# A stack of spectral and token-mixing layers on one Trainium2 core: the last layer's first product, by seven products of quarters

## The chip, the cores and the metric

One core of one Trainium2 chip runs the whole program. Its engines have their own instruction queues and work at the same time: TensorE (PE in the profile; its weight loads are PEld) multiplies matrices, VectorE (DVE) and ScalarE (ACT) do elementwise work, GpSimd (POOL) does some elementwise work and issues transfers, SyncE (SP) only issues transfers. A transfer (DMA) moves data between the chip's memory and the on-chip SBUF. Matmuls write PSUM, which has here four buffers. The metric is the device time of one execution in microseconds, lower is better.

## The reference

Two kinds of layer alternate, A B A B, on x of 2048 tokens by 640 channels. Each adds to x.

```python
def _A_ref(x, w_r, w_i):
    X = rfft2(x); X = X * (w_r + 1j * w_i)
    return irfft2(X, s=(S, D))
def _B_ref(x, w1, b1, w2, b2):
    h = _layernorm(x, axis=-1)
    u = jnp.einsum("bsd,sf->bdf", h, w1) + b1
    u = _gelu(u)
    y = jnp.einsum("bdf,fs->bds", u, w2) + b2
    return y.transpose(0, 2, 1)
x = x + _A_ref(_layernorm(x), A_w_r, A_w_i)
x = x + _B_ref(_layernorm(x), B_w1, B_b1, B_w2, B_b2)
x = x + _A_ref(_layernorm(x), A_w_r, A_w_i)
x = x + _B_ref(_layernorm(x), B_w1, B_b1, B_w2, B_b2)
```

S = 2048, D = 640, F = 1728. All is float32. The two B layers use the same weights. The first product of a B layer is w1 transposed (1728 x 2048) by h (2048 x 640), the second w2 transposed (2048 x 1728) by the GELU of it.

## The kernel before

The kernel gets float32 accuracy out of float16 matmuls: every operand is a high part (float16 of the scaled value) and a low part (float16 of the rest), and `mm3` multiplies high by high, high by low and low by high: three matmuls of 128 x 128 weights by 128 x 320 columns. High parts come from ScalarE, low parts (one subtraction) from VectorE.

`b1st` is the first B layer, `b2nd` the last. The 2048 tokens are 16 row blocks (NJ), the 1728 features 14 tiles of 128 (NFT; tile 13 holds its 64 features twice, so that two matmuls do for three), and the 640 channels two halves of 320. The first product goes tile by tile: per tile 16 row blocks x 2 halves x 3 = 96 matmuls, for tile 13 64. `wload` asks SP for a tile's weights in two transfers of 512 KB, `wsplit` makes the parts, `scan1` and `scale1` (first layer only) find the scale: ScalarE squares and sums the raw tile, VectorE reduces, TensorE adds over partitions.

In `b2nd` SEQ gives the order of the tiles: 0, 7, 6, 13, 1, 8 and so on, so that tiles t and t + 7 follow each other. `both_high` has the first two tiles' products with high parts of h go out early, in gaps of the stage before (`a2`, which makes h, `hf` in float32 and `hh` its high part); the low parts `hl` follow from VectorE. After each tile come bias and GELU, and `usplit` makes the parts of u.

The second product of the last layer (from `PQ`) is already done by quarters, after Strassen and Winograd: for tiles d and d + 8 of the output, the weights are a 2 x 2 block matrix A11, A12, A21, A22 and u a block matrix B11 to B22, and seven products (four sums S1 to S4 of quarters of A, four sums T1 to T4 of quarters of B) do for eight. VectorE forms the S sums (`form`), `hi` and `lo` the parts, three products ahead; `evict` adds a product from PSUM to the results.

The order of the work is the order in which it is written where `self.pin` is set (`Pin`, line 59, is the one line that the profile shows for nearly all operations); elsewhere a planner may move operations by its own estimate. The SP queue works in order: a transfer that must wait for a buffer holds up those behind it. `push` and `pop` open and close pools of SBUF; a tile laid over an older one waits for the older one's last use.

Of the kernel before, what the change touches and what calls it, by code (L numbers as in the profile page):

```python
# [21 lines left out]
NQ = 8  # L22
# [7 lines left out]
SEQ = [t + 7 * i for t in (0, 6, 1, 2, 3, 4, 5) for i in range(2)]  # L30
# [36 lines left out]
class Layers:  # L67
# [41 lines left out]
    def setup(self):  # L109
# [17 lines left out]
        self.s2, self.c2 = (base.tile([128, NQ], F32, name=f"{a}p") for a in "sc")  # L127
        self.second, self.nr = False, 3
# [299 lines left out]
    def a1(self, first):  # L428
# [4 lines left out]
        self.hh = {j: ph.tile([128, 2, 320], F16, name=f"hh{j}_{self.n}") for j in HA}  # L433
# [262 lines left out]
    def a2(self, li):  # L696
# [4 lines left out]
        self.wp[1] = self.push("wb", side=self.sp)  # L701
        ph = self.push("hf", side=self.sp)
        self.hf = [ph.tile([128, 2, 320], F32, name=f"hf{j}_{self.n}") for j in range(NJ)]
# [159 lines left out]

    def b1st(self, li):
# [10 lines left out]
        self.wsplit(1, hi=False)  # L875
        self.wload(2)
# [226 lines left out]
    def usums(self, f, fs, *names):  # L1103

        B11, B12, B21, B22 = (f[:, i] for i in range(4))
        T1, T2, T3, T4 = (fs[:, i] for i in range(4))
        q = {"T1": (T1, B12, B11), "T2": (T2, B22, T1), "T3": (T3, B22, B12), "T4": (T4, B21, T2)}
        for n in names:
            a, b, c = q[n]
            self.V.tensor_tensor(a, b, c, op=ALU.subtract)  # L1110

    def b2nd(self, li):
# [6 lines left out]
        V, T = self.V, self.T  # L1119
        mm = self.PE.matmul  # L1120
        ADD, SUB, MUL = ALU.add, ALU.subtract, ALU.mult
        ph = self.push("h", side=self.sq)
        for j in range(NJ):
            if j not in HA:
                self.hh[j] = ph.tile([128, 2, 320], F16, name=f"hh{j}_{self.n}")
                T.activation(self.hh[j], self.hf[j], AF.Copy)
        self.pin = True
        self.wsplit(1, hi=False)
        self.h = []
        for j in range(NJ):  # L1130
            self.h.append((self.hh[j], ph.tile([128, 2, 320], F16, name=f"hl{j}_{self.n}")))
            V.tensor_tensor(self.h[j][1], self.hf[j], self.hh[j], op=SUB)
        V.tensor_tensor(self.s2, self.st[1][:, :NQ], self.st[1][:, NQ:], op=ALU.min)
        V.tensor_tensor(self.c2, self.ct[1][:, :NQ], self.ct[1][:, NQ:], op=ALU.max)
        self.pin = False
# [3 lines left out]
        px = self.push("px", side=self.sp)  # L1139
        pu = self.push("u", side=self.sp)  # L1140

        u = [pu.tile([128, 2, 7, 320], F16, name=f"u{f}_{self.n}") for f in range(7)]
        p = self.push("b1", side=self.sq)
        for m in (2, 3, 4, 5):
            self.wload(m)

        def ahead(m):

            self.wload(m + 4)
            if m + 1 < NFT:  # L1150
                self.wopen(m + 1)


        PQ = ("A11", "B11"), ("S1", "T1"), ("S2", "T2"), ("S3", "T3"), ("A12", "B21"), ("S4", "B22"), ("A22", "T4")
        UB = {a: i for i, a in enumerate(("B11", "B21", "B22", "T1", "T2", "T3", "T4"))}
        ops = [(d, *q) for d in range(NQ) for q in PQ]
        NP = len(ops)
        places = [(px, f"wo{i}") for i in range(3)] + [(q, a) for q in self.wp for a in ("wh", "wl")]
        src, wo = {}, {}

        def raw(d, a):
            return self.wraws[NFT + 2 * d + int(a[1]) - 1][int(a[2]) - 1]

        def form(n):

            if n >= NP:
                return
            d, a, _ = ops[n]
            if a[0] == "A":
                src[n] = raw(d, a)  # L1170
                return
            s = src[n] = self.t(px, [128, 7, 128], F32, a, 1)
            x, y, op = {
                "S1": ((d, "A21"), (d, "A22"), ADD), "S2": (n - 1, (d, "A11"), SUB),
                "S3": ((d, "A11"), (d, "A21"), SUB), "S4": ((d, "A12"), n - 3, SUB),
            }[a]
            x, y = (src[q] if isinstance(q, int) else raw(*q) for q in (x, y))
            V.tensor_tensor(s, x, y, op=op)

        def hi(n):  # L1180
            if n >= NP:
                return
            q, tag = places[n % 7]
            w = self.t(q, [128, NJ, 128], F16, tag, 1).rearrange("p (a b) c -> p a b c", a=2)[:, :, :7]
            wo[n] = w
            T.activation(w[:, 0], src[n], AF.Identity, scale=self.s2[:, ops[n][0]:][:, :1])

        def lo(n):
            if n >= NP:
                return  # L1190
            w = wo[n]
            V.scalar_tensor_tensor(w[:, 1], src[n], self.s2[:, ops[n][0]:][:, :1], w[:, 0], op0=MUL, op1=SUB)
# [54 lines left out]
        for m in range(NFT):  # L1247
            t, k = SEQ[m] % 7, SEQ[m] // 7
            if m < 2:
                ps, run = pss[m], rest(m, pss[m], w[m])  # L1250
                if m:
                    self.wopen(2)
# [449 lines left out]
```

## Time and profile before

| | us |
|---|---|
| median of 3 runs (1027.93 to 1029.49) | 1028.31 |
| the profiled execution | 1028.95 |
| its span | 1027.2 |
| TensorE busy | 986.3 |
| VectorE busy | 725.5 |
| ScalarE busy | 571.2 |
| GpSimd busy | 265.7 |

In the rows of the profile stand the start in us from the span's start, the duration, the engine, the line, the operation, what it writes and reads, and how many; in brackets the idle time before it and what ended it. Rows of groups give the count, the total, the mean in ns and the idle time before. The chain is the work that ended last, followed back from the end. PEclk is the clock that TensorE was granted, 1.00 in all of the last layer. The last layer's first product lies at about 683 to 864 us, its first matmuls in gaps of the stage before; the second product runs from there to the end.

### The profile page before, as it was taken

How to read it: one execution, taken by the hardware profiler on the slowest of the kernel's cores; microseconds unless marked ns; L12 is line 12 of the kernel's file. 1: busy time of each engine (PE TensorE's matmuls, PEld its weight loads, DVE VectorE, ACT ScalarE, POOL GpSimd, SP SyncE). 2: the span in 40 equal slices, each digit the busy share in tenths (PEclk: the TensorE clock that was granted, in tenths of full speed). 3: DMA queues.
4: the chain of work that ended last, by engine and by line, in shares of the span. 5: the costliest groups of instructions: out<-in, count | busy, mean ns of one | idle time of the engine just before them, and what ended most of it. 6: DMA issues, size and time to landing. Idle time of an engine off the chain costs nothing.

```text
span 1027.2 us, 20943 instructions
## 1 busy us (share of the span) xinstructions
PE 986.3 (96%) x8379; PEld 735.7 (72%) x8379; DVE 725.5 (71%) x1422; ACT 571.2 (56%) x874; POOL 265.7 (26%) x438
## 2 busy tenths in 40 slices
PE   4889999999999999999998999999999999999998
PEld 3768777677777777777776787776777777777776
DVE  7968978954333956666666797897655564988885
ACT  5847768675554556555542575774544454544541
POOL 6927857500000002222222675780000000000000
PEclk9589999999999999999999999999999999999999
DMA  7855356522222264444312644756322232445511
GB/s 230 277 173 168 116 167 222 207 83 99 77 77 74 72 233 155 138 135 123 124 55 86 214 125 130 223 177 210 108 82 83 72 109 77 141 154 175 164 44 52
DMA packets 55738, 139.48 MB, mean 136 GB/s; under 512 B 6461, under 2 KB 12249, under 8 KB 55641
## 3 DMA queue, kind: packets, MB, share of 16 engines
q1 hardware_dynamic: 54200, 131.97, 40.1%
q0 software_dynamic: 1440, 6.17, 2.0%
q8 instruction: 66, 1.08, 0.4%
q14 instruction: 32, 0.25, 0.1%
HBM read 115.05 MB, written 23.07 MB: 134 GB/s over the span
## 4 chain that ended last, share of the span: by engine, by line
PE 76%; DVE 13%; POOL 3%; issue 3%; DMA 2%; ACT 2%; SPq 0%; POOLq 0%; DVEq 0%; ACTq 0%
PE ps L59 76%; DVE st L59 2%; POOL xt L59 2%; DVE xt L59 2%; DVE f L59 1%; DVE Yl L59 1%; DVE s1l L59 1%; DVE hl L59 1%; DVE ta L59 1%; ACT eh L59 1%; DVE el L59 1%; DMA rest<-s1l 1%; POOL r L59 1%; DVE tb L59 1%; DMA stk<-rest 1%
## 5 line engine op out<-in xcount | busy, mean ns | idle before, releaser
L59 PEld LDWEIGHTS <-wh 128*128 128x128 f16 x2992 | 289.7, 98 | 113.4 <-issue 1.8
L59 PEld LDWEIGHTS <-wl 128*128 128x128 f16 x1616 | 157.9, 98 | 62.2 <-DVE wl L59 0.9
L59 PE MATMUL ps<-hh,wh 128*128 128x320 f16 x896 | 186.6, 299 | 0.7 <-ACT hh L59 0.7
L59 PE MATMUL ps<-hl,wh 128*128 128x320 f16 x896 | 184.7, 299 | 0.0
L59 PE MATMUL ps<-hh,wl 128*128 128x320 f16 x832 | 171.4, 299 | 0.6 <-DVE wl L59 0.6
L59 DVE SCALAR_TENSOR_TENSOR wl<-raw,s,wh 128x1024 f16<-128x1024 f32 (+2 forms) x88 | 105.4, 1202 | 87.4 <-ACT wh L59 87.3
L59 PE MATMUL ps<-uh,wl 128*128 128x320 f16 x448 | 133.1, 299 | 0.0
L59 PE MATMUL ps<-ul,wh 128*128 128x320 f16 x448 | 133.1, 299 | 0.0
L59 ACT ACTIVATE wh<-raw,s 128x1024 f16<-128x1024 f32 (+2 forms) x92 | 94.7, 1047 | 68.4 <-PE ps L59 61.6
L59 PE MATMUL ps<-uh,wh 128*128 128x320 f16 x416 | 124.3, 299 | 0.0
L59 ACT ACTIVATE junk<-raw 128x896 bf16<-128x896 f32 (+1 forms) x60 | 59.6, 994 | 46.5 <-DMA raw<-w 46.4
L59 POOL TENSOR_TENSOR r<-v,mh 128x1 f32<-128x1 f32 x64 | 37.4, 584 | 132.2 <-DVE nm L59 122.6
L59 PE MATMUL ps<-tDi,Yh 128*128 128x322 f16 x320 | 71.3, 300 | 0.2
L59 PE MATMUL ps<-u,wo 128*128 128x320 f16 x504 | 69.9, 299 | 0.0
L59 DVE TENSOR_TENSOR f<-eo 128x256 f32<-128x256 f32 (+1 forms) x124 | 39.1, 368 | 38.8 <-POOL eo L59 38.1
L59 PEld LDWEIGHTS <-wo 128*128 128x128 f16 x504 | 49.3, 98 | 19.1
L59 POOL TENSOR_TENSOR xt<-xt,ec 128x320 f32<-128x320 f32 x64 | 52.4, 841 | 32.8 <-DVE xt L59 32.6
L59 PE MATMUL ps<-ph,tS 128*128 128x321 f16 (+2 forms) x288 | 59.6, 289 | 1.3 <-DVE tb L59 1.3
L59 ACT ACTIVATE z<-xt,nb,r 128x640 f32<-128x640 f32 x31 | 28.5, 919 | 55.8 <-POOL z L59 43.5
L59 DVE BATCH_NORM_STATS2 st<-xt 128x6 f32<-128x320 f32 x126 | 55.3, 481 | 5.7 <-DMA xt<-x 4.6
L59 PE MATMUL ps<-tM,f 128*128 128x128 f32 x160 | 39.5, 426 | 19.8 <-DVE f L59 19.8
L59 POOL TENSOR_TENSOR eo<-z 128x320 f32<-128x320 f32 x62 | 53.3, 880 | 17.1 <-ACT z L59 15.1
(174 smaller groups left out, 1877.0 us busy)
## 6 DMA issues: line engine op xcount, KB each, us to landing
raw<-w SPq DMA_DIRECT2D x56, 512.0 KB
xt<-x SPq DMA_DIRECT2D x79, 320.0 KB
w<-w SPq DMA_DIRECT2D x48, 321.0 KB
x<-xt SPq DMA_DIRECT2D x47, 320.0 KB
raw<-w SPq DMA_DIRECT2D x32, 448.0 KB
raw<-w2z SPq DMA_DIRECT2D x32, 448.0 KB
out<-xt SPq DMA_DIRECT2D x15, 320.0 KB
tIM<-tIM POOLq DMA_DIRECT2D x8, 512.0 KB, 5.6
```

The costliest lines, as they stand in the source:

```text
L59: i = f(*a, **k)
```

## The change

The first product of the last layer goes by quarters too. Tile 6 and tile 13 (SEQ is now those two) go as before. The other twelve make six pairs (d, d + 7), each with seven products of 8 row blocks x 3 = 24 matmuls on 320 columns. The quarters A11, A12 and A22 are not loaded as float32 and split: the first layer stores their parts, which it makes anyway, in the chip's memory (`wstore`: both halves of tiles 0 to 5, which are A11 and A12, and the second half of tiles 7 to 12, which is A22), and `fetch` brings them back in one transfer of 512 KB. The sums of weights are made by transfers: SP loads one quarter (`begin`), and GpSimd issues transfers that add others to it in place (`more`). S1 is A21 + A22; when its parts are made, A11 is added to the same buffer, which gives S2, and then A12, which gives S4. S3 is A11 + A21. The signs are taken up by T1 to T4, which VectorE makes in place in `hf` (`tsum`), with parts from `thi` and `tlo`. FIRST, NEXT and LAST1 set the order of the 42 products; `first`, `last` and `stage` hold what goes with each. The loads of w2 for output pair 1 move behind the first product's end, ahead of the first x rows on SP.

```diff
...
-SEQ = [t + 7 * i for t in (0, 6, 1, 2, 3, 4, 5) for i in range(2)]
+SEQ = [6, 13]
...
+        self.s1p, self.c1p, self.c1n = (base.tile([128, 7], F32, name=f"{a}p1") for a in "scn")
+        self.wst = {
+            t: self.dram.tile([128, 2, 2, 8, 128] if t < 6 else [128, 2, 8, 128], F16, name=f"wst{t}")
+            for t in range(NFT - 1) if t != 6
+        }
...
                 V.scalar_tensor_tensor(l, raw, sc, h, op0=ALU.mult, op1=ALU.subtract)
+    def wstore(self, m):
+        if m not in self.wst:
+            return
+        for k, w in enumerate(self.w[m]):
+            q = w.rearrange("p (c b) f -> p c b f", c=2)
+            self.nc.sync.dma_start(*((self.wst[m][:, :, k], q) if m < 6 else (self.wst[m][:, k], q[:, 1])))
...
         self.wsplit(1, hi=False)
+        self.wstore(0)
+        self.wstore(1)
         self.wload(2)
...
             for c in range(2 if m + 1 < NFT + NJ else 0):
                 self.wsplit(m + 1, (c,))
+                if c and m + 1 < NFT:
+                    self.wstore(m + 1)
                 yield
...
+        self.wr[1] = self.push("wr", side=self.sq)
+        px = self.push("px", side=self.sq)
         ph = self.push("h", side=self.sq)
-        for j in range(NJ):
-            if j not in HA:
-                self.hh[j] = ph.tile([128, 2, 320], F16, name=f"hh{j}_{self.n}")
-                T.activation(self.hh[j], self.hf[j], AF.Copy)
-        self.pin = True
-        self.wsplit(1, hi=False)
-        self.h = []
-        for j in range(NJ):
-            self.h.append((self.hh[j], ph.tile([128, 2, 320], F16, name=f"hl{j}_{self.n}")))
...
-        self.pop("hf")
-        self.nr = 4
-        self.wr[1:] = (self.push(a, side=self.sp) for a in ("wr", "wr2", "wr3"))
...
-        for m in (2, 3, 4, 5):
-            self.wload(m)
...
+        hhb, hlb = (ph.tile([128, 8, 2, 320], F16, name=f"{a}b{self.n}") for a in ("hh", "hl"))
+        hl0, hl1 = (q.tile([128, 8, 320], F16, name=f"{a}{self.n}") for q, a in ((ph, "hl0"), (hx, "hl1")))
+        TT = {a: [pt.tile([128, 8, 320], F16, name=f"{a}{b}{self.n}") for b in "hl"] for a in ("T1", "T2", "T3", "T4")}
+        for j in range(8, NJ):
+            T.activation(hhb[:, j - 8], hf[j], AF.Copy)
...
+        P1 = {"A11": "B11", "S1": "T1", "S2": "T2", "A12": "B21", "S3": "T3", "S4": "B22", "A22": "T4"}
+        P2 = {"A11": "B11", "S1": "T1", "S2": "T2", "S3": "T3", "A12": "B21", "S4": "B22", "A22": "T4"}
+        ND = 6
+        FIRST = "A11.0 A12.0 A11.1 A12.1 S1.0 S2.0 S3.0 S4.0 A22.0 S1.1 S1.2 A11.2 S2.1 S3.1 A22.1 S4.1 A12.2 S2.2 S3.2 A22.2 S4.2"
+        NEXT, LAST1 = "S1 A11 A12 S2 S3 A22 S4", "S1 A11 A12 S2 S3 S4 A22"
+        ops = [(int(q[-1]), q[:-2], P1[q[:-2]]) for q in FIRST.split()]
+        ops += [(d, q, P1[q]) for d in range(3, ND) for q in (NEXT if d < ND - 1 else LAST1).split()]
+        N1 = len(ops)
+        at = {(d, a): n for n, (d, a, _) in enumerate(ops)}
+        ops += [(d, *q) for d in range(NQ) for q in P2.items()]
...
+        places = [(px, "wo0"), (px, "wo1"), (self.wp[0], "wl"), (self.wp[1], "wl"), (self.wp[0], "wh"), (self.wp[1], "wh")]
+        w1 = lambda d, a: A["w1"][d + 7 * (a[1] == "2")][:, 8 * int(a[2]) - 8:8 * int(a[2])]
+        w2 = lambda d, a: A["w2z"][d + NQ * (a[1] == "2")][:, 7 * int(a[2]) - 7:7 * int(a[2])]
+        def raw(pool, tag, n, q):
+            return self.t(pool, [128, 8, 128], F32, tag, n)[:, :q]
+        def begin(d, a):
+            pool, tag = (self.wr[1], "Sa") if a == "S1" else (self.wr[0], "raw")
+            cur[d, a] = raw(pool, tag, 2, 8)
+            nc.sync.dma_start(cur[d, a], w1(d, "A21" if a == "S1" else "A11"))
+        def more(d, a, b):
+            G.dma_start(cur[d, a], w1(d, b), accum_op=ADD)
+        def place(n, k):
+            q, tag = places[n % len(places)]
+            w = self.t(q, [128, NJ, 128], F16, tag, 1)
+            w = wo[n] = w[:, :2 * k].rearrange("p (a b) c -> p a b c", a=2)
+            return w
+        def fetch(n):
+            if n < N1 and ops[n][1][0] == "A":
+                d, a, _ = ops[n]
+                nc.sync.dma_start(place(n, 8), self.wst[d][:, int(a[2]) - 1] if a[1] == "1" else self.wst[d + 7])
...
         def hi(n):
...
-            q, tag = places[n % 7]
-            w = self.t(q, [128, NJ, 128], F16, tag, 1).rearrange("p (a b) c -> p a b c", a=2)[:, :, :7]
-            wo[n] = w
-            T.activation(w[:, 0], src[n], AF.Identity, scale=self.s2[:, ops[n][0]:][:, :1])
+            d, a, _ = ops[n]
+            if n < N1:
+                if a[0] == "A":
+                    return
+                src[n] = cur[d, "S3" if a == "S3" else "S1"]
+            elif a[0] == "A" and n not in src:
+                form(n)
+            w = place(n, 8 if n < N1 else 7)
+            T.activation(w[:, 0], src[n], AF.Identity, scale=scale(n))
...
         def lo(n):
-            if n >= NP:
+            d, a, _ = ops[min(n, NP - 1)]
+            if n >= NP or n < N1 and a[0] == "A":
                 return
             w = wo[n]
-            V.scalar_tensor_tensor(w[:, 1], src[n], self.s2[:, ops[n][0]:][:, :1], w[:, 0], op0=MUL, op1=SUB)
-        def prep(m):
+            V.scalar_tensor_tensor(w[:, 1], src[n], scale(n), w[:, 0], op0=MUL, op1=SUB)
+            if n < N1 and a in ("S1", "S2"):
+                more(d, "S1", "A11" if a == "S1" else "A12")
...
+        def tsum(a, c, W=V):
+            j, k = slice(4 * c, 4 * c + 4), slice(8 + 4 * c, 12 + 4 * c)
+            B11, B12, B21, B22 = hfa[:, j, 0], hfa[:, j, 1], hfa[:, k, 0], hfa[:, k, 1]
+            o, x, y = {"T1": (B12, B12, B11), "T2": (B22, B22, B12), "T3": (B11, B22, B11), "T4": (B21, B21, B22)}[a]
+            W.tensor_tensor(o, x, y, op=SUB)
...
+        def thi(a):
             for c in range(2):
-                if m + 1 < NFT:
-                    self.wsplit(m + 1, (c,))
-                yield
+                T.activation(TT[a][0][:, 4 * c:4 * c + 4], tsrc(a, c), AF.Copy)
+        def tlo(a):
+            for c in range(2):
+                j = slice(4 * c, 4 * c + 4)
+                V.tensor_tensor(TT[a][1][:, j], tsrc(a, c), TT[a][0][:, j], op=SUB)
+        def hlow(c):
+            j = slice(4 * c % 8, 4 * c % 8 + 4)
+            if c < 2:
+                V.tensor_tensor(hl0[:, j], hfa[:, j, 0], hha[:, j, 0], op=SUB)
+                V.tensor_tensor(hl1[:, j], hfa[:, j, 1], hha[:, j, 1], op=SUB)
+            else:
+                V.tensor_tensor(hlb[:, j], hfa[:, 4 * c:4 * c + 4], hhb[:, j], op=SUB)
...
+        def product(n):
+            d, a, b = ops[n]
+            o = bank[d, a] = self.big()[:, 0, :320]
+            w = wo[n]
+            for j in range(8):
+                self.mm3(o, (w[:, 0, j], w[:, 1, j]), operand(b, j), j == 0, j == 7)
...
+        for d in range(ND):
+            i = {a: at[d, a] for a in P1}
+            for q in P1:
+                if i[q] < N1 - 1:
+                    first[i[q] + 1].append(lam(evict, d, q))
...
+        for d in range(1, ND):
+            n, k = at[d, "S1"], at[d, "S3"]
+            stage[max(n - 6, 0)].append(lam(begin, d, "S1"))
+            stage[max(n - 5, 0)].append(lam(more, d, "S1", "A22"))
+            stage[max(k - 7, 0)].append(lam(begin, d, "S3"))
+            stage[max(k - 6, 0)].append(lam(more, d, "S3", "A21"))
+        def load2(d, a, pool=None, tag=None, n=2):
+            raws[d, a] = raw(pool, tag, n, 7)
+            nc.sync.dma_start(raws[d, a], w2(d, a))
+        for n, a, pool, tag in (
+            (N1 - 9, "A21", self.wr[1], "Sa"), (N1 - 9, "A22", self.wr[0], "raw"), (N1 - 5, "A11", self.wr[0], "raw"),
+            (N1 - 4, "A12", self.wr[1], "Sa"),
+        ):
+            stage[n].append(lam(load2, 0, a, pool, tag))
...
+        self.pin = True
+        fetch(0)
+        fetch(1)
+        begin(0, "S1")
+        more(0, "S1", "A22")
+        self.wsplit(1, hi=False)
+        begin(0, "S3")
+        more(0, "S3", "A21")
...
+        for js in (early, late):
+            prod(pss[0], wh0, hhigh, js, start=True)
+            prod(pss[0], wl0, hhigh, js)
+            prod(pss[1], wh1, hhigh, js, start=True)
+        fetch(2)
+        fetch(3)
+        hlow(0)
+        hlow(1)
+        for i, w in enumerate((wh0, wh1)):
+            prod(pss[i], w, hlows, low)
+        product(0)
+        hlow(2)
+        hlow(3)
+        for i, w in enumerate((wh0, wh1)):
+            prod(pss[i], w, hlows, high, stop=True)
+        for a in ("T1", "T2"):
+            for c in range(2):
+                tsum(a, c)
+        thi("T1")
+        hi(4)
+        tlo("T1")
+        lo(4)
+        thi("T2")
+        tlo("T2")
+        self.pop("hx")
+        p = self.push("b1", side=self.sq)
+        pr = self.push("br", side=self.sp)
+        f = pr.tile([128, 4, 320], F32, name=f"fr{self.n}")
+        q0, q1 = (pr.tile([128, 2, 320], F32, name=f"qr{k}{self.n}") for k in range(2))
+        t0, t1 = SEQ
+        pv, bb, cc = pss[0][:, :, :320], self.b1[:, t0:t0 + 1], self.ct[0][:, t0:t0 + 1]
+        T.activation(f[:, A2], pv, AF.Identity, scale=cc, bias=bb)
+        T.activation(q0, pv, AF.Square, scale=cc, bias=bb)
+        pv, sw = pss[1][:, :, :320], f[:, A4]
+        T.activation(sw[:64], pv[64:], AF.Copy)
+        T.activation(sw[64:], pv[:64], AF.Copy)
+        V.tensor_tensor(sw, pv, sw, op=ADD)
...
+        for n in range(1, N1):
+            product(n)
+            for e in first[n]:
+                e()
+            if n == 2:
+                hi(5)
+                lo(5)
+            if n > 2:
+                hi(n + 3)
+                lo(n + 3)
+            for e in last[n]:
+                e()
+            for e in stage[n]:
+                e()
+            fetch(n + 4)
+        f5, q2 = fs[D5], q5[1][:, 0]
+        evict(D5, "A22")
...
         self.pop("b1")
+        self.pop("T")
         self.pop("h")
-        self.pop("ha")
         p = self.push("b2", side=self.sq)
...
+        for a in ("A21", "A22", "A11", "A12"):
+            load2(1, a, p, "raw", 8)
         xload(0)
         xbias(0)
...
+            if i in (3, 5) and d + 2 < NQ:
+                for a in ("A11", "A12") if i == 3 else ("A21", "A22"):
+                    load2(d + 2, a, p, "raw", 8)
...
```

More of the change, by code (lines that the diff above doesn't have):

```diff
@@ L1155, in b2nd @@
-        UB = {a: i for i, a in enumerate(("B11", "B21", "B22", "T1", "T2", "T3", "T4"))}
-        ops = [(d, *q) for d in range(NQ) for q in PQ]
-        NP = len(ops)
[L1158 to L1164, printed above, removed]
+        pt = self.push("T", side=self.sq)
+        hx = self.push("hx", side=self.sq)
```

323 lines of the change are left out of this document (187 added, 136 removed).

## The prediction

> **What bounds the kernel now.** I read the head of the page first, then the chain that ended last, then the last layer's stretches by window.
>
> ```profile
> span 1027.2 us, 20943 instructions
> PE 986.3 (96%) x8379; PEld 735.7 (72%) x8379; DVE 725.5 (71%) x1422; ACT 571.2 (56%) x874; POOL 265.7 (26%) x438
> ```
> ```profile
> 197.27 358.44 PE ps L59 x2784
> ...
> 703.39 3.96 DMA raw<-w
> ...
> 712.13 311.52 PE ps L59 x2292
> ```
> ```profile
> core 0: us, PE busy (x) PEld busy (x) DVE busy (x) ACT busy (x) POOL busy (x), PEclk, DMA share, GB/s
> 704.00:712.00 8.00, 7.53 (x56) 5.10 (x53) 2.25 (x6) 4.55 (x6) 0.00 (x0) 1.00 0.86 273
> 712.00:725.00 13.00, 12.87 (x95) 9.30 (x96) 9.50 (x15) 7.64 (x12) 0.00 (x0) 1.00 0.63 236
> 712.00:868.00 156.00, 155.87 (x1148) 112.30 (x1149) 88.71 (x114) 77.61 (x98) 0.00 (x0) 1.00 0.32 103
> ```
> From 712.13 us to the end the chain is matrix products and nothing else, at granted clock 1.00. The first product of the last layer keeps TensorE busy without a break but for 0.47 + 0.13 = 0.60 us at 704 to 725. So a matmul removed there is worth its full pace, and a new wait costs its full length.
>
> **What goes.** The pace, from the start of one tile's second row block to the start of the next tile's first (15 blocks of 6):
>
> ```profile
> 712.42 0.43 PE L59 MATMUL ps<-hh,wh 128*128 128x320 f16 x2
> ...
> 724.64 0.43 PE L59 MATMUL ps<-hh,wh 128*128 128x320 f16 x2
> ...
> 875.14 3.02 PE L59 MATMUL ps<-u,wl 128*128 128x320 f16 x21
> 878.00 3.02 PE L59 MATMUL ps<-u,wh 128*128 128x320 f16 x21
> ```
> 12.22 us / 90 = 0.1358 us. The second product, which already works by quarters, goes at 2.86 / 21 = 0.136, so one matmul per loaded weight is not slower. Before: 13 tiles x 96 + 64 (the doubled tile) = 1312. After: tile 6 with 96, tile 13 with 64, and 6 pairs x 7 products x 8 row blocks x 3 = 1008; together 1168. 144 x 0.1358 = **19.55 us less**. The 0.60 us of idle goes too: its load waited for space that the new order does not need so early.
>
> **The new start.** This is where it is paid for. Rows of the old start:
>
> ```profile
> 689.83 2.47 DVE L59 SCALAR_TENSOR_TENSOR wl<-raw,s,wh 128x1024 f16<-128x1024 f32 x2
> 692.21 11.85 DVE L59 TENSOR_TENSOR hl<-hf,hh 128x640 f16<-128x640 f32 x16
> ```
> ```profile
> 695.34 0.43 PE L59 MATMUL ps<-hh,wh 128*128 128x320 f16 x2 [0.19 <-ACT hh L59]
> ```
> ```profile
> L59 DVE SCALAR_TENSOR_TENSOR wl<-raw,s,wh 128x1024 f16<-128x1024 f32 x22 | 28.3, 1284 | 44.4 <-ACT wh L59 44.4
> L59 ACT ACTIVATE wh<-raw,s 128x1024 f16<-128x1024 f32 x22 | 25.2, 1144 | 40.3 <-PE ps L59 35.0 <-issue 5.2
> L59 DVE SCALAR_TENSOR_TENSOR xt<-ps,cp,xt 128x320 f32<-128x320 f32 x32 | 17.6, 551 | 20.7 <-ACT m L59 11.7 <-PE ps L59 8.9
> L59 DVE SCALAR_TENSOR_TENSOR wh<-raw,s,wl 128x512 f16<-128x512 f32 x2 | 1.5, 752 | 0.0
> L59 DVE TENSOR_TENSOR sw<-ps,sw 128x640 f32<-128x640 f32 x1 | 0.8, 825 | 2.9 <-ACT sw L59 2.9
> ```
> ```profile
> tIM<-tIM POOLq DMA_DIRECT2D x8, 512.0 KB, 5.6
> ```
> ```profile
> 254.43 0.33 SPq L834 DMA_DIRECT2D raw<-w  x1
> ```
> ```profile
> 258.05 1.06 ACT L59 ACTIVATE junk<-raw 128x1024 bf16<-128x1024 f32 x1 [1.76 <-DMA raw<-w]
> ```
> TensorE as if nothing were late: the last high parts are in hand at 695.34, 18 matmuls to 697.8, 32 with the first eight low blocks to 702.1, product 0 (24, 3.26 us) to 705.4, the other 32 to 709.7, then one product per 3.26 us: product 4 (S1 of pair 0) at 719.5.
>
> VectorE, 0.74 us per 640 elements (11.85 / 16): split of tile 13 (1.5) and five small scalars (0.8) from 689.83 to 692.1; low parts to 704.0, each just ahead of its use; sums T1, T2 (5.9) to 709.9; low T1 (2.96) to 712.8; low part of S1 (1.28) to 714.1; low T2 to 717.1; the add for tile 13 to 717.9; sums T3, T4 to 723.8; one eviction (0.55) to 724.4. The bank of tile 13 is free only at 717.9, and product 3 wants it at 716.2: **1.7 us**. S1 then runs 721.2 to 724.4.
>
> Now the accumulating transfers. A quarter is 512 KB. No row has one; call a its time from issue to landing. Ends: 3.6 us (a plain load issued by SP, 254.43 to 258.05) and 11.2 (twice POOL's row of 5.6, a read and an add one after the other). I take 7.1: POOL's 5.6 and one more passage of the bytes, 0.52 MB at about 360 GB/s (rows below), since it is nearest to a single POOL transfer. With 7.1: S1's low part at 714.1, A11 is added by 721.2, S2's high part is ready in time, and its low part waits for VectorE: 725.6. S2 starts 725.3 instead of 724.4 (**0.9**; the low part is first read 0.27 us into a product). T3's low half, then S3's low part at 729.9: **1.0**. A12 is issued at 725.6, lands 732.7, high 1.14 and low 1.28: 735.1, S4 wanted at 732.9: **1.9**. While ScalarE and VectorE stand at this wait, evictions and T4 queue behind it; four PSUM banks cover them.
>
> SP has its own queue. It loads A21 of pair 2 into the buffer that S4 of pair 0 frees, at 735.1, and behind that load stands the fetch of product 8's stored quarter: issued 735.5, 3.6 plus 1.5 behind the other transfer, landing 740.5, wanted at 738.1: **2.4**. The same load then needs its own accumulation: 735.1 + 3.6 + 7.1 + 2.4 = 748.2 for S1 of pair 2 (product 10), wanted 747.0: **0.9**. POOL, idle here, queues a pair's additions behind the wait for the pair before; the next user is product 9, 10 us on. Sum of the start: **8.8 us**. The same steps give 4.4 with a = 3.6 (S4's and product 10's waits gone, the fetch 0.8) and 19.2 with a = 11.2 (1.7 + 3.0 + 1.0 + 6.1 + 2.4 + 5.0).
>
> The Trainium skill, DMA: Bandwidth & Descriptors, section Anatomy of one DMA, gives a transfer by this path 2.0 us plus its bytes at 436 GB/s. For 512 KB that makes 3.2 us as an estimate, against POOL's measured 5.6; the start would then cost a little under 4.4, and the sum would end near 1014. The measured row decides.
>
> **The six pairs in steady order.** A product lasts 3.26 us, a pair 168 x 0.1358 = 22.8 us. S1 to S2 and S2 to S4 are three products, 9.8 us; a link is a + 1.14 + 1.28 = 9.5 with my a. With 11.2 it is 13.6, which eats 3.8 of the lead twice per pair; the lead is three products less 2.4, and the plain quarters give it back. I take 0, up to 3. VectorE's rows:
>
> ```profile
> L59 DVE SCALAR_TENSOR_TENSOR q<-q,f 128x640 f32<-128x640 f32 x13 | 10.7, 825 | 8.6 <-ACT q L59 8.6
> L59 DVE SCALAR_TENSOR_TENSOR u<-fs,su,u 128x960 f16<-128x960 f32 x6 | 7.3, 1218 | 1.8 <-ACT u L59 1.8
> L59 DVE TENSOR_TENSOR fs<-f,fs 128x320 f32<-128x320 f32 x14 | 6.8, 489 | 0.2
> L59 DVE SCALAR_TENSOR_TENSOR u<-f,su,u 128x640 f16<-128x640 f32 x7 | 6.2, 880 | 0.0
> ```
> Per pair: 4 low parts 5.1, evictions 5 x 0.55 + 2 x 0.49 = 3.7, GELU 4 x 0.83 = 3.3, sums 4 x 0.49 = 2.0, low parts of the split u 0.55 + 0.88 + 1.6 = 3.0: 17 of 22.8 us.
>
> Bytes per pair: three stored quarters, two plain loads, four accumulations.
>
> ```profile
> 716.00:718.00 2.00, 2.00 (x17) 1.43 (x16) 2.00 (x4) 1.33 (x3) 0.00 (x0) 1.00 0.88 317
> 718.00:720.00 2.00, 2.00 (x17) 1.45 (x15) 1.97 (x5) 1.27 (x2) 0.00 (x0) 1.00 0.97 356
> ```
> That is 360 GB/s at full share, 1.46 us per quarter. Five plain: 7.3 us. An accumulation holds the engines at least 1.46; twice that if the old value is read as well: 7.3 + 11.7 = 19.0 of 22.8, hidden.
>
> The Trainium skill, Collectives: The Full Stack, section The bandwidth ceiling, says that an adding transfer reads two sources through one ring and so runs at half the rate of a copy. It is the rule that speaks against this change; by it the pair stands at those 19.0 us, the transfers are five sixths of the time, and the sum stays. No row before shows it.
>
> **The change-over to the second product.** Four w2 quarters now go out on SP ahead of the x rows of block 0, into space that the last products free.
>
> ```profile
> 854.15 8.26 SPq L1327 DMA_DIRECT2D xt<-x  x6
> ```
> ```profile
> 869.93 1.53 ACT L59 ACTIVATE xt<-xt,b2s 128x640 f32<-128x640 f32 x2
> ```
> ```profile
> 863.73 8.31 PE L59 MATMUL ps<-u,wo 128*128 128x320 f16 x60
> ```
> Before, x was asked for 9.6 us ahead of the second product's first matmul. Now 1.84 + 0.66 MB leave when S4 of the last pair ends, 3.3 us ahead: x lands some 6 to 8 us into the product, ScalarE stands at the bias (1.53) and then forms product 4's weights (about 2.7), which TensorE wants 11.4 us in. I take **1.0**; 0 if the space is free earlier, 3.5 if only at the stage's end.
>
> **The first layer's stores.** 9 MB more, 24 transfers on SP. At its start two tiles' stores (2 MB) stand ahead of the load of tile 2.
>
> ```profile
> 202.97 0.16 DVE L59 TENSOR_REDUCE sqb<-sq 128x1 bf16<-128x2 f32 x1
> ```
> ```profile
> 205.69 0.17 PE L59 MATMUL ps<-sqb,ones 128*128 128x1 bf16 x1
> ```
> The load lands 2 to 4 us later; this reduce may move 2.7 us before TensorE waits: 0.3, at worst 3. Later each tile's load follows 1 MB of store; ScalarE's scan of the load ends some 3 us later per 13.03 us tile, with a tile's lead: 0.
>
> **Sum.** -19.55 - 0.60 + 8.8 + 1.0 + 0.3 = -10.05 us. The profiled execution took 1028.95 us (span 1027.2): 1018.9. The median of the runs, 1028.31, is 0.64 lower: **1018** us.
>
> **Rivals.** *The start is covered* (a near 3.6, nothing else late): -19.55 - 0.60 + 4.4 = -15.75, 1012.5. For it: POOL has nothing else to do and VectorE no wait of its own; against: POOL's row of 5.6 without any addition.
> *Accumulations are slow* (a near 11): -20.15 + 19.2 + 1 + 0.3 = +0.4, 1028 to 1029; near 9, halfway, 1023.
> *The transfers become the bound* (the other side). If an accumulation holds the engines for k plain passages, a pair takes 7.3 + 4 x 1.46 k: beyond k = 2.65 that is over 22.8, and at k = 3 it is 24.8, +2.0 x 6 = 12, which takes the gain away. At k = 3.5: 27.7, +29, 1047. For it: nothing in the trace has an addition, and share was 0.97 with plain loads alone; against: two reads need only k = 2.
> *The first layer pays*: 3 us at its start and 3 on the way, 1024.
>
> **How the numbers follow.** About 0.2%, 2 us, is what a measurement of this kernel tells from no change. The likeliest case, a between 5 and 9, 1013 to 1023: 0.50. Covered start: 0.13. Slow accumulations: 0.15, of which half end within 0.2%. First layer pays: 0.05. Transfers bound: 0.17, slower. Faster 0.76, same 0.07, slower 0.17. The likeliest case's own range is 1012 to 1024; with the ends of a and the change-over's 3.5 the range is 1010 to 1031.
>
> **What will show it.** The products on TensorE from 709 to 748: gaps ahead of products 3, 5, 6, 7, 8 and 10, released by VectorE, VectorE, VectorE, ScalarE's or VectorE's wait for a transfer, a fetch, and again a transfer. 1008 matmuls at 0.136. POOL's transfers, 24 of them, near 7 us. DMA share near 0.8 in steady pairs; at 1.0 with TensorE waiting in every pair, the last rival is right. First layer: no idle of TensorE between 197 and 555. The prediction is wrong if gaps recur in pairs 3 to 5, or if S1 to S4 of pair 0 are not where the start waits.

## The result, and the profile after

The changed kernel takes 1040.97 us (median of 4 runs, 1038.15 to 1043.51) against 1028.9 for the kernel before in the same comparison (4 runs): ratio 1.0114, 95% interval 1.0084 to 1.0145. It is 1.1% slower; the forecast was 1018. The profiled execution below took 1038.15 us, the lowest of the four.

Head of the page after: the removed matmuls are gone, 8379 - 8235 = 144.

```profile
span 1036.4 us, 20858 instructions
...
PE 974.6 (94%) x8235; PEld 722.8 (70%) x8235; DVE 765.1 (74%) x1470; ACT 582.8 (56%) x896; POOL 285.4 (28%) x462
```

Where the span's +9.2 us came from is read on TensorE, mainly at two places. First, its instructions in pair 0 (start, duration, then in brackets the idle time ahead and what ended it):

```profile
729.27 0.45 PE L59 MATMUL ps<-T3h,wo 128*128 128x320 f16 x2 [0.57 <-DVE wo L59]
...
733.76 0.45 PE L59 MATMUL ps<-hhb,wo 128*128 128x320 f16 x2 [0.88 <-DVE wo L59]
...
740.84 0.30 PE L59 MATMUL ps<-T4h,wl 128*128 128x320 f16 x1 [3.92 <-ACT f L59]
...
742.77 0.74 PE L59 MATMUL ps<-T4h,wl 128*128 128x320 f16 x2
```

The last matmul of product 7 starts at 736.62 and product 8 (`T4`) at 740.84, released by an eviction on ScalarE, not by a transfer. Then pairs of matmuls take 0.74 us instead of 0.43: TensorE's clock has dropped (granted 0.69 from 740 to 745 us). Second, the change-over:

```profile
857.12 2.72 PE L59 MATMUL ps<-u,wo 128*128 128x320 f16 x18
864.52 0.30 PE L59 MATMUL ps<-u,wo 128*128 128x320 f16 x1 [4.69 <-ACT u L59]
865.11 4.35 PE L59 MATMUL ps<-u,wo 128*128 128x320 f16 x20 [0.29 <-DVE u L59]
873.92 0.43 PE L59 MATMUL ps<-u,wo 128*128 128x320 f16 x1 [4.46 <-ACT u L59]
874.84 0.69 PE L59 MATMUL ps<-u,wo 128*128 128x320 f16 x2 [0.50 <-DVE u L59]
...
1026.89 5.87 PE L59 MATMUL ps<-u,wo 128*128 128x320 f16 x42
```

The last row in the kernel before, for comparison:

```profile
1020.62 3.02 PE L59 MATMUL ps<-u,wl 128*128 128x320 f16 x21
```

The second product runs from 857.12 to 1032.76, 175.6 us. Before it ran from 863.73 to 1023.64, 159.9. Without new waits the first product would have ended 19.55 + 0.60 us earlier than before, at 843.6; it ended at 857.1. So +13.5 lies ahead of the change-over, +15.7 at it, and -20.15 + 13.5 + 15.7 is the +9.2 of the span, within the rounding. Of the 13.5, 2.0 are there before any product by quarters: product 0 starts at 704.14, not at the forecast's 702.1. Most of them come from the first layer, as its own experiment below shows.

What ScalarE and VectorE do at the change-over:

```profile
848.34 1.15 ACT L59 ACTIVATE wh<-Sa,sp 128x1024 f16<-128x1024 f32 x1 [2.16 <-DMA Sa<-w]
...
860.80 0.56 ACT L59 ACTIVATE f<-v,b1s 128x320 f32<-128x320 f32 x1 [4.66 <-DVE v L59]
...
873.05 0.81 ACT L59 ACTIVATE u<-f,su 128x640 f16<-128x640 f32 x1
...
879.09 1.53 ACT L59 ACTIVATE xt<-xt,b2s 128x640 f32<-128x640 f32 x2
```
```profile
872.10 0.54 DVE L59 SCALAR_TENSOR_TENSOR f<-ps,c,f 128x320 f32<-128x320 f32 x1
```

The eviction of the first product's last bank (A22 of pair 5) starts at 872.10, 15 us after its product ended. The operand T1 that TensorE waits for is made at 873.05, behind it. Both engines take their instructions in written order, and 15 us is the time of more than four products; the x rows (879.09) are not what TensorE waits for in these rows. The chain that ended last shows how they came to be late: from 774.13 to 848.34 most of it is accumulating transfers, each started when the split of the sum before is done.

```profile
774.13 10.76 DMA Sa<-w
...
787.75 7.18 DMA Sa<-w
...
798.31 8.94 DMA Sa<-w
...
833.63 5.96 DMA Sa<-w
839.63 2.81 issue
842.46 5.79 DMA Sa<-w
848.34 1.16 ACT wh L59
...
884.53 148.25 PE ps L59 x1090
```

The stretches by window (busy time of TensorE, its weight loads, VectorE, ScalarE, GpSimd; then TensorE's granted clock, the share of the sixteen DMA engines, GB/s) and the transfers from issue to landing:

```profile
760.00:800.00 40.00, 38.95 (x285) 27.45 (x284) 30.68 (x43) 22.39 (x31) 5.26 (x6) 1.00 0.70 176
800.00:850.00 50.00, 49.98 (x368) 35.39 (x365) 34.41 (x47) 27.05 (x38) 6.13 (x7) 1.00 0.86 205
850.00:860.00 10.00, 8.98 (x64) 6.20 (x65) 9.90 (x15) 3.31 (x4) 0.00 (x0) 1.00 0.64 210
860.00:870.00 10.00, 4.65 (x21) 2.64 (x21) 7.46 (x13) 5.31 (x10) 0.00 (x0) 0.83 1.01 398
870.00:880.00 10.00, 5.30 (x23) 2.75 (x22) 7.17 (x14) 5.09 (x10) 0.00 (x0) 0.66 0.01 4
```
```profile
Sa<-w POOLq DMA_DIRECT2D x18, 512.0 KB, 6.2
...
raw<-w POOLq DMA_DIRECT2D x6, 512.0 KB, 9.7
```

The steady pairs are nearly as forecast: TensorE full at 0.86 of the DMA engines from 800 to 850, and 1.05 us idle at 760 to 800. TensorE stands at 850 to 880 while VectorE is busy 9.90, 7.46 and 7.17 of 10.

### The profile page after: what moved, and what is told of

Its sections match the earlier page's. It is cut to its first block, busy times and chain, and to the rows that moved or that the text cites. A ratio compares the mean times of both kernels' runs of the same rounds, so it can differ in the third digit from the quotient of the medians.

```text
span 1036.4 us, 20858 instructions
## 1 busy us (share of the span) xinstructions
PE 974.6 (94%) x8235; PEld 722.8 (70%) x8235; DVE 765.1 (74%) x1470; ACT 582.8 (56%) x896; POOL 285.4 (28%) x462
## 3 DMA queue, kind: packets, MB, share of 16 engines
q8 instruction: 64, 1.05, 0.4%
## 5 line engine op out<-in xcount | busy, mean ns | idle before, releaser
L59 PEld LDWEIGHTS <-wh 128*128 128x128 f16 x2602 | 251.2, 98 | 101.6 <-DVE wh L59 2.6
L59 PEld LDWEIGHTS <-wo 128*128 128x128 f16 x756 | 73.9, 99 | 45.4 <-issue 10.9
L59 PE MATMUL ps<-hl,wh 128*128 128x320 f16 x504 | 104.1, 299 | 0.0
L59 DVE SCALAR_TENSOR_TENSOR wl<-raw,s,wh 128x896 f16<-128x896 f32 (+2 forms) x64 | 74.6, 1169 | 35.5 <-ACT wh L59 35.5
L59 ACT ACTIVATE wh<-raw,s 128x896 f16<-128x896 f32 (+2 forms) x68 | 67.3, 1012 | 20.5 <-PE ps L59 18.9
L59 PE MATMUL ps<-u,wo 128*128 128x320 f16 x420 | 61.3, 305 | 9.9 <-ACT u L59 9.1
L59 PE MATMUL ps<-hha,wh 128*128 128x320 f16 x304 | 61.5, 299 | 1.1 <-ACT wh L59 1.1
L59 PE MATMUL ps<-tDi,Yl 128*128 128x322 f16 x192 | 55.7, 299 | 1.5 <-DVE Yl L59 1.5
```

Of the source, the lines that this page charges most:

```text
L59: i = f(*a, **k)
```

## The experiments

The theories. A: the last pair's sums wait for two accumulating transfers, which puts ScalarE and VectorE behind. B: these two engines' tail behind the last product (evictions, GELU, splits, sums of w2) is longer than what TensorE has to do beside it, even with no transfer late. C: the loads of w2 or x for the second product are late. P: product 8 waits for a PSUM bank whose eviction stands behind other work on ScalarE; against it the forecast's reason, the fetch of its stored quarter.

For each kernel, "second product" is the time from its first matmul to its last on TensorE (159.9 before, 175.6 after), read as above. Ratios are to the kernel before in the same comparison.

**The last pair without its additions.** In `lo`, the additions of A11 and A12 for pair 5 are left out, so that its S2 and S4 are the sum S1 again.

```
-            if n < N1 and a in ("S1", "S2"):
+            if n < N1 and a in ("S1", "S2") and d < ND - 1:
```

> Leaves out the additions of A11 and A12 in the last pair (pair 5), so its S2 and S4 are S1 over again and nothing waits for those two transfers; all other work stays. Theory A (in the last pair S4 follows S2 by two products only, the two waits for added transfers put ScalarE and VectorE three products behind, and the change-over to the second product pays for it): the change-over, 15.8 us longer than before in the changed kernel, falls to about 6; time near 1032. Theory B (VectorE and ScalarE have more work in the last five products than TensorE gives time for, waits or not): 1039 to 1041. Theory C (the w2 and x loads at the change-over): 1041.

1035.19 us, ratio 1.005 (1.0032 to 1.0067). From 804 to the end of the first product TensorE no longer waits, but the second product still takes 171.3 us:

```profile
860.60 2.88 PE L59 MATMUL ps<-u,wo 128*128 128x320 f16 x20 [0.29 <-DVE u L59]
869.40 0.43 PE L59 MATMUL ps<-u,wo 128*128 128x320 f16 x1 [5.93 <-ACT u L59]
```

So A holds for 4.3 of the 15.7; 11.4 us of loss stay with no late sum in the last pair, and the time lies between what A and B gave.

**No additions at all.** All 24 accumulating transfers are left out, so every sum is its first quarter alone.

```
-            G.dma_start(cur[d, a], w1(d, b), accum_op=ADD)
+            pass
```

> Leaves out all 24 accumulating transfers; every sum of weights is then its first quarter alone. Theory A: as with the last pair alone, and also the waits of about 1 us before products 6, 7, 13 and 22 of the first product go, perhaps 4 us: near 1028. Theory B: 1036 to 1038, since only the start gains. If the transfers were the bound anywhere, DMA share near 1.0 would go with TensorE's waits.

1026.09 us, ratio 0.996 (0.9945 to 0.9974). TensorE keeps its exact pace from product 14 on, the gap ahead of product 8 is still 2.31 us behind ScalarE's eviction, and the second product takes 169.2 us:

```profile
851.30 5.46 PE L59 MATMUL ps<-u,wo 128*128 128x320 f16 x39
861.69 0.43 PE L59 MATMUL ps<-u,wo 128*128 128x320 f16 x1 [4.93 <-ACT u L59]
```

That is 9.3 us lost at the change-over with no such transfer at all: B. The time is below what either theory gave, because the additions cost about as much ahead of the change-over (it starts 5.8 us earlier) as at it (6.4). Even so the change would gain only some 4 us of the 20 that its matmuls are worth.

**The same transfers, overwriting.** The 24 transfers stay, on the same queue, with the same waits and bytes, but they overwrite the buffer; the sums are left out again.

```
-            G.dma_start(cur[d, a], w1(d, b), accum_op=ADD)
+            G.dma_start(cur[d, a], w1(d, b))
```

> The 24 additions are made as plain transfers by the same queue: same bytes, same waits, but they overwrite the buffer instead of adding to it (so the sums of weights are left out of the computation). If the adding itself is what costs (reading the old value too), the transfers land in about 5.3 us and the pairs' share of the DMA engines falls well below that of the changed kernel (0.67 to 0.89), and the time comes most of the way to the 1026 of the kernel without these transfers: 1028 to 1033. If it is the place of a transfer in the chain, whatever it does there, the time stays at 1037 to 1041.

1027.98 us, ratio 0.9983 (0.9973 to 0.9994): most of the way to the kernel without them. The lists of DMA issues and of the queues (packets, MB, share of sixteen engines' span), first of this kernel:

```profile
Sa<-w POOLq DMA_DIRECT2D x18, 512.0 KB, 4.8
...
raw<-w POOLq DMA_DIRECT2D x6, 512.0 KB, 6.8
```
```profile
q0 software_dynamic: 4896, 18.76, 5.7%
```

Of the changed kernel, and of the kernel before:

```profile
q0 software_dynamic: 4896, 18.76, 8.8%
```
```profile
q0 software_dynamic: 1440, 6.17, 2.0%
```

Landing falls by 1.4 and 2.9 us. In a chain of two per pair that decides whether the engines keep up: the second product takes 169.2 us here, exactly as with no transfers, so the adding itself costs 6.4 of the 15.7 at the change-over, and 1.3% of the time (ratio 1.0114 to 0.9983, 13 us) in all.

**Another order at the end.** S1 of pair 5 is moved into pair 4, and S2 to S4 are three products apart.

```
...
+        TAIL = "S1.4 A11.4 A12.4 S2.4 S3.4 S1.5 A22.4 S4.4 A11.5 S2.5 A12.5 S3.5 S4.5 A22.5"
...
```

> All work kept; the first product of the last pair, S1, is moved two products ahead, between products of pair 4, and S2 before A12, so that S1 to S2 is four products and S2 to S4 three instead of two. Theory A: the last wait falls by 3 to 6 us and the change-over with it, time 1032 to 1037. Theory B: 1040 to 1042, unchanged.

1042.51 us, ratio 1.0119. The second product is shorter (172.1 us), but S1 of pair 5 is now late itself, and the first product ends at 862.2 instead of 857.1. The delay is moved, not removed.

**GELU of tiles 6 and 13 later.** From steps 4 and 5 to steps 6 to 8.

```
-        last[4] += [lam(thi, "T4"), lam(tlo, "T4"), g0(1), g0(2), dup1, g0(3), g1(1)]
-        last[5] += [g1(2), g1(3)]
+        last[4] += [lam(thi, "T4"), lam(tlo, "T4")]
+        last[6] += [g0(1), g0(2), dup1, g0(3)]
+        last[7] += [g1(1), g1(2)]
+        last[8] += [g1(3)]
...
```

> All work kept; GELU of tiles 6 and 13 moves from steps 4 and 5 to steps 6 to 8, so that ScalarE evicts product 4 from PSUM before it. Theory P (product 8 waits 4.1 us for the PSUM buffer of product 4, because ScalarE does that GELU in turns with VectorE first; the slow clock after the gap costs another 1.7): gap gone, time 1034 to 1037. Rival, the prediction's step (product 8 waits for the fetch of its stored quarter behind the load of pair 2): gap stays, 1041.

1042.07 us, ratio 1.0118. The gap ahead of product 8 is gone, which settles P: it was the bank, not the fetch. But product 10, S1 of pair 2, now waits:

```profile
745.51 0.31 PE L59 MATMUL ps<-T1h,wh 128*128 128x320 f16 x1 [2.81 <-ACT wh L59]
746.83 0.45 PE L59 MATMUL ps<-T1h,wh 128*128 128x320 f16 x2 [0.88 <-DVE wh L59]
```

**More work for TensorE at the change-over.** Products 0 to 3 of the second product run without tile 5 first (in the changed kernel only 2 and 3), and the last eviction and the weights of product 3 move ahead of the last GELU.

```
...
-            late = n in (2, 3)
+            late = n < 4
...
```

> At the change-over TensorE has 39 matmuls that do not need the last pair's GELU (products 0 and 1 of the second product, short of tile 5), then it stands. Here products 0 to 3 all run without tile 5 first, 72 matmuls, and the last pair's last eviction and the weights of product 3 are moved ahead of the last GELU. Theory B (the last pair's tail on VectorE and ScalarE is simply longer than the work TensorE has beside it): 33 more matmuls, 4.5 us, run in the wait, and the second product loses about 11 us instead of 15.8: 1035 to 1037. Theory C (the weights or x of the second product are late as well): products 2 and 3 wait themselves, nothing is gained, 1041.

1039.96 us, ratio 1.0099 (1.0084 to 1.0115), second product 176.3: nothing gained. The added matmuls wait for weights, then for a bank:

```profile
864.07 0.45 PE L59 MATMUL ps<-u,wo 128*128 128x320 f16 x2 [2.51 <-ACT wo L59]
...
883.83 8.69 PE L59 MATMUL ps<-u,wh 128*128 128x320 f16 x42 [4.98 <-DVE xt L59]
```

Weights, operands and evictions all come from the same two late engines. The reason given beforehand for "nothing gained", late loads, is not what the rows show: from 852 to 890 us no instruction on either engine waits for a load, so C is out, here as in the changed kernel.

**Three sums on GpSimd.** The sums S1, S3, S2 of w2's block 0.

```
-            V.tensor_tensor(s, get(x), get(y), op=op)
+            (G if d == 0 and a != "S4" else V).tensor_tensor(s, get(x), get(y), op=op)
```

> The changed kernel with the three sums of w2 quarters of block 0 (S1, S3, S2, 3.2 us of VectorE in the last four products) made by GpSimd, which is idle there. If VectorE's and ScalarE's work behind the last products is what the change-over waits for, the 15.8 us lost there shrink by about those 3.2 us, and by up to 5 with the clock: 1036 to 1038. If the waits for the last additions alone set it, nothing changes: 1041.

1040.65 us, ratio 1.0101 (1.0086 to 1.0116). The second product is 2.3 us shorter (173.3), as B has it, but the first ends later (861.8), with waits at S3 of pair 5; the sum is unclear. VectorE's bare sum of work is then not the whole of B. The order in which the two engines wait for each other probably counts too; this kernel does not show it apart.

**The first layer's stores later.** Stores of tiles 0 and 1 go out behind the loads of tiles 2 to 4.

```
-        self.wstore(0)
-        self.wstore(1)
         self.wload(2)
...
         for m in (3, 4):
             self.wload(m)
+        self.wstore(0)
+        self.wstore(1)
```

> The first layer's stores of tiles 0 and 1 leave after its loads of tiles 2 to 4 instead of ahead of them. If those stores delay the load of tile 3, the two waits of TensorE at 213 and 215 us (1.11 and 0.60 us in the changed kernel) go, and if nothing gives them back the time falls by up to 1.7 us: 1039.3. In the changed kernel the first layer ended only 0.3 us later than before in spite of those waits, so 0.3 us, not measurable, is the rival.

1040.49 us, ratio 1.01 (1.0085 to 1.0115). TensorE's waits in the first layer's start remain, 0.81 and 0.60 us. This order hardly moves a transfer: three of the four stores go out before 181 us in both kernels, and the fourth only moves from between the two loads of tile 2 to behind them. So it does not test the stores. What the load of tile 3 waits for can be read without it. SP's own waits for VectorE's low parts from 192 to 207 us (total, times, longest), of the kernel before, the changed kernel and this one, and ScalarE's scan of that load in the changed kernel:

```profile
SPq L834 <- DVE hl L59: 3.7, 4, 1.1
```
```profile
SPq L844 <- DVE hl L59: 10.6, 1, 10.6
```
```profile
SPq L844 <- DVE hl L59: 10.9, 1, 10.9
```
```profile
209.49 1.06 ACT L59 ACTIVATE junk<-raw 128x1024 bf16<-128x1024 f32 x1 [8.04 <-DMA raw<-w]
```

That load goes into the space of `hf`. Before, `hf` was sixteen tiles, one per row block, and a load waited at most 1.1 us for a low part. The change makes it one tile, which T1 to T4 are taken from:

```
-        self.hf = [ph.tile([128, 2, 320], F32, name=f"hf{j}_{self.n}") for j in range(NJ)]
...
+        self.hfa = ph.tile([128, NJ, 2, 320], F32, name=f"hf{self.n}")
+        self.hf = [self.hfa[:, j] for j in range(NJ)]
```

So the load waits until VectorE has made the last low part, at 205.28 us. ScalarE scans it at 209.49 instead of 202.22, its evictions and splits stand behind the scan, and TensorE waits 1.11 and 0.60 us (213.28 and 214.60). Nothing gives these back: TensorE's sum over partitions comes at 204.91, 0.78 us earlier than before (205.69), the last transform ahead of the last layer at 686.59, 1.98 later than before (684.61). The 0.3 us of the expectation was read on ScalarE (694.22 against 693.94), which waits for GpSimd there. No kernel here has the new products with `hf` in sixteen tiles.

**The last pair by plain products.** Pair 5 takes eight products of quarters instead of seven (A11 B11, A12 B21, A11 T1, A12 B22, A21 B11, A22 B21, A21 T1, A22 B22): 24 matmuls more, no sum, and results that are complete earlier.

```
...
+        Q5 = (("A11", "B11"), ("A12", "B21"), ("A11", "T1"), ("A12", "B22"))
+        R = (("A21", "B11"), ("A22", "B21"), ("A21", "T1"), ("A22", "B22"))
...
+            ops += [(ND - 1, *q) for q in Q5 + R]
...
```

> The last pair is made by eight plain products of quarters (three stored quarters and A21 split on the spot; A11 T1 + A11 B11 stands for A11 B12), so 24 matmuls more, +3.3 us, but no accumulating transfer in the last pair and only one quarter of GELU behind the last product. Theories A and B together (the tail of the seven-product pair is the loss): the change-over falls from 15.8 to 1 to 4 us, 1028 to 1032. Theory C (loads for the second product, or its own start): the loss stays over 10, 1038 to 1044.

1034.61 us, ratio 1.0049 (1.0035 to 1.0063). The second product takes 166.0 us: 9.6 of the 15.7 are gone, for 3.3 paid. 6.1 are left where 1 to 4 were expected, so the tail of the seven-product pair is most of the loss and not all of it.

**First and last pair by plain products.**

```
...
+        if 0 in PLAIN:
+            ops = [(0, *q) for q in Q0 + R] + ops
...
```

> As the one before, and the first pair by eight plain products too: another 24 matmuls, +3.3 us, and the first accumulating sums are wanted eight products later. If the start's waits (about 11.7 us in the changed kernel) come from sums that are wanted before they can be made, they fall to 1 to 4 us, and the time is 5 to 7 us below the one before: 1022 to 1027, under the kernel before. If they come from VectorE's work on the operand sums T1 to T4 and the GELU of tiles 6 and 13, they move to the next pair as they did when the GELU was put later, and the time is 3 us above the one before.

1025.1 us, ratio 0.9957 (0.9942 to 0.9971): faster than the kernel before, and 9.5 us below the last one although it has 24 matmuls more. In the profiled executions the products from 704 to 770 us take 2.2 us more than 0.1358 us per matmul here, and 13.4 more in the last one. Two rows of the windows, and two of the three waits that are left at the change-over:

```profile
705.00:760.00 55.00, 53.17 (x391) 37.88 (x390) 46.61 (x50) 33.89 (x41) 5.21 (x6) 1.00 0.50 117
760.00:800.00 40.00, 40.00 (x296) 28.81 (x295) 30.86 (x43) 21.23 (x28) 5.26 (x6) 1.00 0.76 190
```
```profile
864.89 0.45 PE L59 MATMUL ps<-u,wh 128*128 128x320 f16 x2 [1.96 <-ACT wh L59]
866.08 4.83 PE L59 MATMUL ps<-u,wh 128*128 128x320 f16 x22 [0.74 <-DVE wh L59]
```

**Its weights earlier.** The splits for products 3 and 4 of the second product go ahead of the last GELU.

```
-        last[N1 - 1] += [lambda: q5.pop(1), half(2, 0, 1, 2, 3)] + split1(1, 1, 2)
+        last[N1 - 1] += [lam(hi, N1 + 3), lam(lo, N1 + 3), lambda: q5.pop(1), half(2, 0, 1, 2, 3)] + split1(1, 1, 2)
...
+        hi(N1 + 4)
         evict8(N1 - 1)
...
```

> The kernel with the first and the last pair plain, with the splits of the weights for products 3 and 4 of the second product placed ahead of the last GELU on ScalarE and VectorE. In that kernel TensorE still loses 5.8 us at the change-over and waits there for exactly these weights (1.96 + 0.74 + 1.18 us, and a lower clock after it). If the order on ScalarE and VectorE is the cause, 3 to 5 us go: 1020 to 1022. If the two engines simply have too much to do, the wait moves to the next thing they make and the time stays at 1024 to 1026.

1026.09 us (1022.86 to 1027.84), ratio 0.9961 (0.9941 to 0.9981): no difference that the intervals show. The wait for weights is gone and another has its place, a bank whose eviction stands behind the last splits on ScalarE:

```profile
868.47 7.37 PE L59 MATMUL ps<-u,wo 128*128 128x320 f16 x42 [3.91 <-DVE xt L59]
```
```profile
865.88 1.53 ACT L59 ACTIVATE xt<-xt,b2s 128x640 f32<-128x640 f32 x2
```

**All of it together**, with the three sums on GpSimd and the stores later.

> First and last pair plain, the weights of products 3 and 4 early, the three sums of w2 quarters on GpSimd, and the first layer's first stores behind its loads. By the sum of the parts: 1 to 2 us under the kernel with early weights, 1018 to 1021. If GpSimd's sums come too late for product 2 of the second product, 1 to 3 us slower than that kernel.

1023.56 us (1021.34 to 1024.17), ratio 0.9932 (0.9918 to 0.9947): 0.7% faster than the kernel before, and the lowest of all that ran, though not the 1018 to 1021 expected. Its second product still takes 164.5 us, 4.6 more than before; the longest wait there is for a bank again:

```profile
868.80 6.02 PE L59 MATMUL ps<-u,wo 128*128 128x320 f16 x42 [2.76 <-DVE xt L59]
```

## Why the prediction was wrong

- **What goes** was right: 144 matmuls fewer, at the old pace. In the steady pairs TensorE keeps that pace from 804 to the last pair.
- **The new start** was sized nearly right, for partly wrong reasons: forecast 8.8, found about 10.0. That TensorE reaches product 4 at 721.53, as the forecast's 719.5 + 1.7 + 0.3 has it, is luck: product 0 was 2.0 late already, and the bank that product 3 was to wait 1.7 for came free at 717.95, as forecast, just before TensorE wanted it (718.27). Products 5, 6 and 7 lose 0.2, 0.9 and 1.0 (forecast 0.9, 1.0, 1.9). Product 8 was to wait 2.4 for a fetch behind another load on SP; it lost 4.1 for a bank, plus 1.7 of lower clock. Product 10 lost nothing (forecast 0.9), and product 13 waited twice, 2.1 together. The forecast listed "evictions and T4 queue behind it; four PSUM banks cover them": they did not.
- **The accumulating transfers**: 6.2 us (9.7 for those into `raw`) against the 7.1 taken. Two reads, k = 2, against 1.86 measured. The rival that the transfers become the bound did not come true: share 0.70 to 0.86 and TensorE full in the middle.
- **The steady order** had an oversight: S2 to S4 was put at three products for every pair. In the last pair it is two, 6.5 us for a link of 9.5 by the forecast and 8.6 by the chain's rows (2.81 + 5.79). ScalarE waits there (848.34, 2.16 us), VectorE behind it, and the lag is carried into the change-over: 4.3 us by the kernel without the last pair's additions. A gap in pair 5 was one of the two signs that the forecast named against itself; the other came in part, since the start's longest wait is at product 8, which has no sum of weights.
- **The change-over to the second product** is the step that failed: forecast 1.0, at most 3.5, found 15.7. It looked at the x rows on SP's queue only. What was not costed is the work on ScalarE and VectorE behind the last product: before, the last thing finished was one tile; now four quarters of results are complete only with the last four products, and their GELU, their splits, the sums of w2 and the weights of the next product stand in one written order on two engines that wait for each other. That alone is 9.3 us (no additions, or overwriting ones), and the late additions bring it to 15.7. How the 9.3 divide among GELU, splits, evictions and the sums of w2 stays open: moving or sparing single pieces (more work for TensorE, the sums on GpSimd, the weights earlier) moved the wait to the next piece.
- **The first layer's stores**: forecast 0.3, found about 2.0, which TensorE carries through the layer after it. "No idle of TensorE" there was wrong, and so was the cause: the load of tile 3 waits for the space of `hf`, which the change made one tile, and not behind the stores. The forecast did not look at that part of its own change.

So the sum -20.15 + 8.8 + 1.0 + 0.3 lacks 14.7 at the change-over, 1.2 at the start, 1.7 in the first layer and some 1.7 in the later pairs. The other 2.8 to the median lie between the profiled execution and the other runs, 1040.5 to 1043.5, and were not taken apart.

## What to carry to other kernels

Where a product is cut into pieces whose results are complete only with the last pieces, cost the engines behind TensorE at the end of the stage as carefully as the start: list what they must do after the last matmul, in written order, against what TensorE can do without it. Here a scheme that saves matmuls with late results paid only in the middle of the stage: plain products for the first and last pair, 6.5 us dearer on TensorE, turned 1.1% slower into 0.4% faster. Where moving one wait only brought up another with the same releasers, reordering gained nothing here, and shortening the chain did. And where several tiles are joined to one, look for what is laid over them: it may now wait for the last use of all.

## What the hardware showed

**TensorE's clock after a wait.** After 3.92 us of idle the matmuls went at 0.74 us per two from 742 to 745 us, 1.7 us lost on top of the wait; after 4.69 and 4.46 us at the change-over 20 matmuls took 4.35 and 4.39 us, against 2.88 in the kernel without the last pair's additions, with granted clocks of 0.83 and 0.66 in those windows. After 3.91 us (the kernel with its weights earlier) the next 42 took 7.37 us instead of 5.87, after 4.98 (more work for TensorE) 8.69; after 2.76 us (everything together) 6.02. But shorter waits were followed by it too: with the first and the last pair plain, waits of 1.96 and 0.74 us came ahead of 22 matmuls in 4.83 us, where 22 took 3.16 at 880.42 in the changed kernel:

```profile
866.20:869.40 3.20, 3.20 (x13) 1.82 (x13) 1.73 (x5) 2.94 (x5) 0.00 (x0) 0.50 1.02 413
```

The Trainium skill, TensorE: Matmul & The Clock Gate, section Part 1: The HAM clock gate, states that the clock halves after an idle window of about 3.4 us and comes back after about as long under load. The slow stretch from 742 to 745 us agrees with that length; as a bound on a single wait 3.4 us does not hold here, since 1.96 us with 0.74 behind it was followed by a halved clock and 2.76 us was not. The waits of 3.9 us and more in these rows cost 1.5 to 2.8 us above their length, which the forecast had not counted.

**What an addition costs the DMA engines.** From the three queue rows above: a plain quarter of 512 KB holds sixteen engines for (5.7% x 1026.7 - 2.0% x 1027.2) / 24 = 1.58 us, an adding one for (8.8% x 1036.4 - 20.5) / 24 = 2.94 us, a ratio of 1.86. The Trainium skill, Collectives: The Full Stack, section The bandwidth ceiling, explains the half rate of ReduceScatter, whose transfers add, by two source reads through one ring; the ratio here is near it, for transfers from the chip's memory that add in SBUF.
